# Bucket bits of seven head pairs: twelve fp32r products become four fp32 products in four column tiles, ten steps earlier

## The chip, the core and the metric

The kernel runs on one core of one Trainium2 chip. The metric is the device time of one execution in microseconds. The kernel before takes 722.88 us, the median of three runs from 721.88 to 723.98.

## The reference

Attention in which a query sees only the keys of its own hash bucket, and then two feed-forward layers of 1536 tokens, 512 channels and 2048 hidden units:

```python
B, H, S, D = 2, 8, 768, 64
q_bits = (einsum('bhsd,dk->bhsk', q, proj) > 0)      # six bits per query
k_bits = (einsum('bhsd,dk->bhsk', k, proj) > 0)      # six bits per key
mask = bucket(q_bits)[:, :, :, None] == bucket(k_bits)[:, :, None, :]
scores = where(mask, D**-0.5 * q @ k.T, -1e9)
x = softmax(scores) @ v                              # then to 1536 x 512
x = square(relu(x @ w_in1)) @ w_out1
out = silu(x @ w_in2) @ w_out2
```

All inputs are fp32, and the result has to be close to fp32 accuracy.

## The kernel before

The 16 heads are taken as 8 pairs. Operands of the large products are split in two fp32r parts, a high part and what is left, and a product of two such operands is written as three products. The mask is put into the score product itself: beside the 64 rows of q and k that belong to the low parts, the second half of each head's operand (`qq[h][:, 1]`, `kk[h][:, 1]`) has 12 rows with bits, six for "bit is set" and six for "bit is not set". On the query side they hold one or zero, on the key side a large negative number or zero, so that each bit in which a query and a key differ adds a large negative number to the score.

**The calendar of the attention.** `lsh_attention_moe_moe` writes one order of all instructions by hand. Its loop runs over steps d from -5 to 98 (line 1243 on). One step makes the scores of one tile of 128 queries (`score_mm`, line 989, four products into one of two PSUM banks-of-two `s`), takes the row maximum of the tile before (`row_max`, 996, and `row_live`, 1000 and 1001, on VectorE), its exponential (`score_exp`, 1009, on ScalarE), transposes two key tiles (`transp`, 1025, six transposes into a ring of three banks `t`), splits them (`t_hi`, a cast on ScalarE, 1030; `t_lo`, a subtraction on VectorE, 1036), and multiplies two earlier ones with v (`av`, 1049 and 1050). Twelve steps are one pair; in what follows d0 = 12 (p - 1) for pair p, whose scores run from step d0+7 (head 0) and d0+13 (head 1). Beside this, `todo[d]` holds what a step issues at its end, `last[d]` what comes after that, and `mid[d]` what VectorE does in its middle, after `row_live`. The engines and the DMA queues take their instructions in order: what SyncE waits for holds back every later DMA of its queue.

**The bits of pairs 1 to 7.** For each pair, q and k (two heads, 128 rows) are loaded (`load_pair`, 741, at d0-13, `load_k`, 744, at d0-6), q is scaled on ScalarE (758, at d0-7), high parts are cast on GpSimd (754, at d0-7 and d0-2) and low parts subtracted there (774, at d0-5 and d0-1). In step d0+5 (5, 17, ..., 77; the table `long`) `bits_mm` (line 789) multiplies with the signed projection: for each half of the 768 columns six fp32r products of 128 rows, 48 output rows and 384 columns, that is the high projection with the high part, the low projection with the high part and the high projection with the low part, for q and for k. They accumulate in 48 rows of two banks, one taken from the scores (`s`), one from the transposes (`t`). Two comparisons on VectorE (`bits_cmp`, 795) turn them into the bits tile `bt`, of which there is one buffer. In such a step the exponential goes ahead of the products with v, since the bits take its bank, and q of a later pair is scaled right after it. `place_bits` (919) then sends 12 rows of `bt` into `qq` and 12 into `kk` by two DMAs on SyncE's queue, for head 0 at the end of step d0+5, for head 1 at step d0+8. The heads' other rows are sent there by `load_head` (764, 766) and `place_lo` (779, 780). Pair 0 makes its bits apart, before step 0 (`first_bits_mm`, 884, `second_bits_mm`, 900).

**The first layer's w_in.** Four tiles of w_in, stored as fp64 words, are made fp32 during the attention: a load (943), an absolute value on ScalarE (950), a limit on GpSimd (954), and three integer operations on VectorE (`w_exp` 958, `w_sign` 962, `w_low` 966). `W_STEPS` names the steps: load, absolute value and limit, then the three. Two raw tiles are used in turn. At the last of the steps of the first two, `wp_put` (973, 974) splits the tile for the feed-forward part.

After the attention a planner orders the two layers; their first products (line 420) need the first x and w_in tiles. The row sums of each pair come back as a tile `rw` (1087), of which there are two buffers.

Of the kernel before, what the change touches and what calls it, by code (L numbers as in the profile page):

```python
# [23 lines left out]
NB = 6  # L24
# [7 lines left out]
WARM = {-4: 5, 0: 1, 1: 1}  # L32
PW = 96
C = float(2.0**36)
# [5 lines left out]
V_LAG = 4  # L40
W_STEPS = ((0, 5, 17, 17, 29), (8, 17, 29, 41, 53), (30, 41, 53, 65, 77), (54, 65, 77, 92, 93))
WA = 4
# [657 lines left out]
def lsh_attention_moe_moe(ctx, tc, kd, qk, qf, fq, v, pc, wi1, wo1, wi2, wo2, out):  # L700
# [27 lines left out]
    pjs = ac.tile([128, PW], F32, name="pjs")  # L728
    pjh = ac.tile([128, PW], F32R, name="pjh")
    pjl = ac.tile([128, PW], F32R, name="pjl")  # L730
    pjd = ac.tile([128, 3, 88], F32R, name="pjd")
    pdx = ac.tile([128, 2, NBR], F32, name="pdx")
    tm = [tmt[:, 2 * i : 2 * i + 2] for i in range(4)]
    mt = ac.tile([128, 4, 4], F32, name="mt")

    pair = {}
# [33 lines left out]
    def split_pair(p, i):  # L770
        t = pair[p]
        if i == 0:
            t["lp"] = a1.tile([128, 2, S], F32R, tag="lp", bufs=2, name=f"lp{p}")
        nc.gpsimd.tensor_tensor(out=t["lp"][:, i], in0=t["r"][i], in1=t["hp"][i].bitcast(F32), op=ALU.subtract)
# [7 lines left out]
    def bits_mm(p):  # L782
        t = pair[p]
        hp, lp = t["hp"], t["lp"]
        ops = [(w[:, 48 * i : 48 * i + 48], x) for i in range(2) for (w, x) in ((pjh, hp[i]), (pjl, hp[i]), (pjh, lp[:, i]))]
        s = ps_s.tile([128, 2, 512], F32, tag="s", name=f"bs{p}")[:, 0], ps_t.tile([128, 512], F32, tag="t", name=f"bt{p}")
        for z in range(2):
            for j, (w, x) in enumerate(ops):
                mm(s[z][0:48, 0:QW], w, x[:, z * QW : (z + 1) * QW], start=j == 0, stop=j == 5)  # L789
        return s  # L790

    def bits_cmp(s, p, z):
        if z == 0:
            pair[p]["bt"] = a1.tile([128, S], F32R, tag="bt", name=f"bt{p}")
        nc.vector.tensor_scalar(
            out=pair[p]["bt"][0:48, z * QW : (z + 1) * QW],
            in0=s[z][0:48, 0:QW],
            scalar1=tm[0][0:48, 0:1],
            scalar2=tm[0][0:48, 1:2],
            op0=ALU.is_gt,  # L800
            op1=ALU.mult,
        )

# [6 lines left out]
    def first_load(h):  # L810
        t = pair[0]
        if h == 0:
            c = ac.tile([128, S], F32, tag="P", bufs=6, name="fc")
            first["c"] = c[:, 0:NFQ]
            first[0, 0] = c[:, NFQ : NFQ + QW], ac.tile([128, S], F32, tag="P", bufs=6, name="fq1")[:, 0:QW]
            k = a1.tile([128, S], F32, tag="ta", bufs=2, name="fk")
            first[0, 1] = k[:, half(0)], k[:, half(1)]
            nc.sync.dma_start(out=c[:, 0 : NFQ + QW], in_=fq)
            nc.scalar.dma_start(out=first[0, 1][0], in_=qf[0, 1, :, half(0)])
            nc.sync.dma_start(out=first[0, 1][1], in_=qf[0, 1, :, half(1)])  # L820
            nc.scalar.dma_start(out=first[0, 0][1], in_=qf[0, 0, :, half(1)])
        else:
            first[1, 0] = a1.tile([128, S], F32, tag="tb", name="fr10")
            first[1, 1] = a1.tile([128, 6, 2, 64], F32, tag="rw", bufs=2, name="fr11").rearrange("p a b c -> p (a b c)")
# [90 lines left out]
    def place_bits(p, h):  # L915
        t = pair[p]
        for n, x in enumerate(("qq", "kk")):
            r = 24 * n + NBR * h
            nc.sync.dma_start(
                out=t[x][h][64 : 64 + NBR, 1, :].bitcast(F32),  # L920
                in_=t["bt"][r : r + NBR].bitcast(F32),
            )

# [13 lines left out]
    def w_load(key):  # L937
        m, io, i = key
        if io:
            weights[key] = raw[i], late[i]  # L940
        else:
            weights[key] = raw[i % 2], ac.tile([128, 512], F32, tag="wi", bufs=2, name=f"wi{i}") if i < 2 else wt[i - 2]
        nc.sync.dma_start(out=weights[key][0], in_=((wi1, wo1), (wi2, wo2))[m][io][i])
# [125 lines left out]
    def norm_rows(p):  # L1069
        ri = sums[p]  # L1070
        nc.vector.reciprocal(out=ri, in_=ri)
        if p == NPAIR - 1:
            w = rows[p] = a1.tile([128, 6, 2, 64], F32, tag="rw", bufs=2, name=f"rw{p}")
            nc.gpsimd.tensor_copy(out=w, in_=ri.rearrange("p (h c) -> p c h", h=2).unsqueeze(3).broadcast_to([128, 6, 2, 64]))
# [9 lines left out]
    def row_get(p):  # L1084
        w = rows[p] = a1.tile([128, 6, 2, 64], F32, tag="rw", bufs=2, name=f"rw{p}")
        for h in range(2):
# [88 lines left out]
    with tc.manual_schedule():  # L1175
# [50 lines left out]
        at(-4, lambda: nc.gpsimd.tensor_tensor(out=pjs, in0=pcr[:, 0:PW], in1=pcr[:, PW:], op=ALU.mult))  # L1226
        at(-4, lambda: nc.gpsimd.tensor_copy(out=pjh, in_=pjs))
        at(-4, lambda: nc.gpsimd.tensor_tensor(out=pjl, in0=pjs, in1=pjh.bitcast(F32), op=ALU.subtract))
        at(-3, scale_q, 1)
# [9 lines left out]
        for d in range(-5, G // 2 + 3):  # L1239
# [17 lines left out]
            elif 0 <= g < G:  # L1257
# [59 lines left out]
def _layout(q, k, v, proj, moe_w_in, moe_w_out, moe2_w_in, moe2_w_out):  # L1317
# [13 lines left out]
    for s in range(2):  # L1331
        for h in range(2):
            for e in range(2):
                r = 24 * s + NBR * h + NB * e
                c = 48 * s + r
                plus = e == s
                pj[64 * h : 64 * h + 64, c : c + NB] = proj
                sg[:, c : c + NB] = 1.0 if plus else -1.0
                at = (TINY if plus else -TINY2, -C if s else 1.0)
                tm[r : r + NB, 0:2] = at  # L1340
                tm[64 + NB * e : 64 + NB * e + NB, 2 + 2 * s : 4 + 2 * s] = at
# [20 lines left out]
```

## Time and profile before

| what | value |
|---|---|
| median of three runs | 722.88 us |
| profiled execution, its own time | 722.25 us |
| span in that profile, first to last instruction | 720.5 us |
| TensorE busy | 714.9 us, 99% of the span |
| VectorE, ScalarE, GpSimd busy | 609.0, 538.8, 257.6 us |
| granted TensorE clock, mean | 0.999 |

Times in rows are microseconds from the start of the span unless marked ns. PE is TensorE, PEld its weight loads, DVE VectorE, ACT ScalarE, POOL GpSimd, SPq the queue of SyncE. In a timeline a row is: start, length, engine, line, operation, out<-in, shapes, count, and in brackets the idle time before it with what ended it. "issue" is idle time for which the profile shows no other cause. Ends of products are modelled, so that two products in a row overlap in the listing; the distance between starts is the better measure.

### The profile page before, as it was taken

The numbers are of one execution on the slowest core, as the hardware profiler recorded it, in microseconds if no ns is written. First come the engines' busy times: TensorE is split into PE (matmuls) and PEld (weight loads), VectorE is DVE, ScalarE is ACT, GpSimd is POOL, SyncE is SP. The second block draws the span as 40 slices with busy tenths as digits, with TensorE's granted clock in tenths as the row PEclk, the third lists the DMA queues.
The fourth block names the chain that finished last, engine by engine and source line by source line (L and its number), as shares of the span: only waits on it lengthen the run. The fifth ranks groups of instructions, "written<-read, shape, count | busy, mean of one in ns | idle before, by whom it ended". The sixth has DMA issues, their size and how long they took to land.

```text
span 720.5 us, 10899 instructions
## 1 busy us (share of the span) xinstructions
PE 714.9 (99%) x3638; PEld 611.8 (85%) x3638; DVE 609.0 (85%) x1106; ACT 538.8 (75%) x1012; POOL 257.6 (36%) x241
## 2 busy tenths in 40 slices
PE   9999999999999999999999999999999999999998
PEld 4999999999999888888888888888788888888886
DVE  6999999999999888886797889988878788888840
ACT  6998898899898897495568569888765945854861
POOL 7645656665546421041331231244204111212300
PEclk9999999999999999999999999999999999999999
DMA  5788898797553555143544742477131332245432
GB/s 173 199 199 172 177 225 168 176 231 173 135 134 86 117 158 120 59 96 95 117 102 103 167 126 74 102 174 179 52 94 58 89 103 84 92 103 117 103 110 95
DMA packets 38824, 92.56 MB, mean 128 GB/s; under 512 B 5608, under 2 KB 10580, under 8 KB 38768
## 3 DMA queue, kind: packets, MB, share of 16 engines
q1 hardware_dynamic: 26304, 67.58, 33.4%
q0 software_dynamic: 12032, 23.79, 18.9%
q8 instruction: 29, 0.48, 0.3%
q10 hardware_dynamic: 432, 0.49, 0.2%
q14 instruction: 27, 0.22, 0.1%
HBM read 52.35 MB, written 3.19 MB: 77 GB/s over the span
## 4 chain that ended last, share of the span: by engine, by line
PE 98%; DVE 1%; ACT 0%; issue 0%; DVEq 0%; ACTq 0%
PE bank L558 36%; PE bank L443 25%; PE s L989 9%; PE t L1025 9%; PE bank L420 7%; PE o L1049 5%; PE o L1050 5%; PE bs L789 1%; PE bt L789 1%; PE warm L980 1%; DVE mt L996 0%; ACT P L1009 0%; PE bs L900 0%; PE bf L884 0%; PE t L1263 0%
## 5 line engine op out<-in xcount | busy, mean ns | idle before, releaser
L558 PE MATMUL bank<-woh,cell 128*128 128x512 f32 (+1 forms) x392 | 119.9, 385 | 0.0
L558 PE MATMUL bank<-cell,woh 128*128 128x512 f32 x384 | 118.4, 389 | 0.0
L1009 ACT ACTIVATE P<-s,mt 128x768 f32<-128x768 f32 x96 | 95.4, 994 | 14.1 <-DVE mt L1001 10.7
L1036 DVE TENSOR_TENSOR tl<-t,th 128x384 fp32r<-128x384 f32 x192 | 104.6, 548 | 0.5 <-ACT th L1030 0.5
L996 DVE TENSOR_REDUCE mt<-s 128x1 f32<-128x768 f32 x96 | 91.4, 952 | 3.2 <-PE s L989 2.4
L1030 ACT CAST th<-t 128x384 fp32r<-128x384 f32 x192 | 81.9, 484 | 8.4 <-PE t L1025 8.1
L558 PEld LDWEIGHTS bank<-woh,cell 128*128 128x128 f32 x392 | 73.1, 188 | 14.7
L989 PE MATMUL s<-kk,qq 76*128 76x384 f32 (+1 forms) x384 | 84.7, 340 | 0.7 <-ACT P L1009 0.5
L558 PEld LDWEIGHTS bank<-cell,woh 128*128 128x128 f32 x384 | 72.1, 188 | 15.2 <-DMA cell<-cell 0.2
L1025 PE MATMUL t<-ident,P 128*128 128x128 f32 x576 | 79.0, 273 | 0.0
L278 DVE TENSOR_TENSOR cell<-bank,cell 128x512 f32<-128x512 f32 x91 | 62.1, 692 | 19.7 <-PE bank L443 15.3
L443 PE MATMUL bank<-xw,wpb 128*128 128x512 f32 x312 | 75.9, 389 | 0.0
L558 PE MATMUL bank<-wol,cell 128*128 128x512 f32 (+1 forms) x196 | 75.4, 385 | 0.0
L558 PE MATMUL bank<-cell,wol 128*128 128x512 f32 x192 | 74.7, 389 | 0.0
L1049 PE MATMUL o<-th,vv 128*128 128x384 f32 x192 | 72.5, 378 | 0.0
L1025 PEld LDWEIGHTS t<-ident,P 128*128 128x128 f32 x576 | 68.0, 140 | 4.6 <-DVE tl L1036 0.2
L989 PEld LDWEIGHTS s<-kk,qq 76*128 76x128 f32 (+1 forms) x384 | 68.0, 188 | 4.1 <-issue 1.6
L443 PEld LDWEIGHTS bank<-xw,wpb 128*128 128x128 f32 x312 | 58.5, 188 | 12.4 <-DVE bank L278 0.3
L1050 PE MATMUL o<-tl,vv 128*128 128x384 f32 x192 | 64.5, 336 | 0.0
L588 ACT COPY yf<-bank 128x512 f32<-128x512 f32 x48 | 27.9, 585 | 34.6 <-PE bank L558 33.9
L450 ACT COPY cell<-bank 128x512 f32<-128x512 f32 x39 | 22.9, 586 | 40.6 <-PE bank L443 38.6
L268 ACT CAST cell<-cell 128x512 fp32r<-128x512 f32 x81 | 48.8, 617 | 2.5 <-DMA cell<-cell 1.3
(198 smaller groups left out, 1480.9 us busy)
## 6 DMA issues: line engine op xcount, KB each, us to landing
raw<-in_dram SPq DMA_DIRECT2D x64, 512.0 KB
cell<-cell POOLq DMA_DIRECT2D x23, 256.0 KB, 3.6
qq<-hq SPq DMA_DIRECT2D x28, 192.0 KB
kk<-in_dram POOLq DMA_DIRECT2D x14, 384.0 KB, 5.8
yf<-cell POOLq DMA_DIRECT2D x21, 256.0 KB, 3.6
vr<-in_dram SPq DMA_DIRECT2D x8, 384.0 KB
ta<-ob SPq DMA_DIRECT2D x31, 96.0 KB
tb<-ob SPq DMA_DIRECT2D x31, 96.0 KB
```

Of the source, the lines that this page charges most:

```text
L278: add("DVE", 0.70, lambda: vec.tensor_tensor(out=val(out), in0=bank[b], in1=val(other), op=ALU.add), [("bank", b), *reads], writes)
L420: mm(bank[b], wpa[n][:, p, 4 * h + j], x[:, q], start=j == 0 and z == 0, stop=j == 3 and z == 2)
L443: mm(bank[b], w[:, p], x[:, q], start=not started and z == 0, stop=z == 2, skip_group_check=started)
L558: mm(bank[b][:, 0:wd], x, y, start=start and i == 0 and z == 0, stop=i == (FB if half is None else 2 * half + 2) - 1 and z == 2, skip_grou ...
L989: mm(s[:, n, 0:QW], t["qq"][h][0:kk, ab, c0 : c0 + 128], t["kk"][h][0:kk, ab, n * QW : (n + 1) * QW], start=ab == 0, stop=ab == 1)
L996: nc.vector.tensor_reduce(out=m[:, 0:1], in_=s[:, :, 0:QW], op=ALU.max, axis=AX.XY, negate=True)
L1009: nc.scalar.activation(out=e.rearrange("p (a b) -> p a b", a=2), in_=s[:, :, 0:QW], func=AF.Exp, scale=m[:, 1:2], bias=m[:, 2:3], accum_ou ...
L1025: nc.tensor.transpose(t[:, j * 128 : (j + 1) * 128], P[u, j][:, kt * 128 : (kt + 1) * 128], ident)
L1030: nc.scalar.copy(out=th, in_=PT[g][0][:, 0:QW])
L1036: nc.vector.tensor_tensor(out=tl, in0=t[:, 0:QW], in1=th.bitcast(F32), op=ALU.subtract)
L1049: mm(o[:, 0:QW], vv, th, start=kt == 0, stop=False)
L1050: mm(o[:, 0:QW], vv, tl, start=False, stop=kt == KT - 1)
```

## The change

It forms the bits of pairs 1 to 7 from q and k as loaded, by four fp32 products per pair, one for each of q and k and each half of the columns. Each writes 24 of 32 output rows of its own at partition 0, 32, 64 or 96 of one bank from the ring `t`. The projection is no longer split, and `pjh` and `pjl` go with the two GpSimd operations that made them. One comparison of 128 partitions and 384 columns makes all bits of the pair; `place_bits` sends each half of the columns by its own DMA, four per head in place of two. The products stand at the end of step d0-2 (step 1 for pair 1), after the scores, the comparison in the middle of step d0-1, and the bits of head 0 are placed at step d0+2.

q and k of a pair are loaded at d0-10 and d0-9. k is cast and split first (d0-4, d0-3), q is scaled in step d0-2 after the bits products, which read it unscaled, then cast and split (d0-2, d0-1). The exponential no longer changes its place in a step with bits. The w_in tiles get a third raw tile `rx` and other steps: only step 41, 92 and 96 still have two of the VectorE operations, and the last tile is finished at step 96. `rw` has one buffer.

```diff
-PW = 96
+PW = 64
-W_STEPS = ((0, 5, 17, 17, 29), (8, 17, 29, 41, 53), (30, 41, 53, 65, 77), (54, 65, 77, 92, 93))
+W_STEPS = ((0, 5, 17, 29, 53), (8, 17, 41, 65, 77), (22, 29, 41, 92, 93), (54, 65, 92, 96, 96))
...
-    pjh = ac.tile([128, PW], F32R, name="pjh")
-    pjl = ac.tile([128, PW], F32R, name="pjl")
+    rx = ac.tile([128, 512], I64, name="rx")
...
     def bits_mm(p):
-        t = pair[p]
-        hp, lp = t["hp"], t["lp"]
-        ops = [(w[:, 48 * i : 48 * i + 48], x) for i in range(2) for (w, x) in ((pjh, hp[i]), (pjl, hp[i]), (pjh, lp[:, i]))]
-        s = ps_s.tile([128, 2, 512], F32, tag="s", name=f"bs{p}")[:, 0], ps_t.tile([128, 512], F32, tag="t", name=f"bt{p}")
-        for z in range(2):
-            for j, (w, x) in enumerate(ops):
-                mm(s[z][0:48, 0:QW], w, x[:, z * QW : (z + 1) * QW], start=j == 0, stop=j == 5)
-        return s
+        o = ps_t.tile([128, 512], F32, tag="t", name=f"bs{p}")
+        for c in range(4):
+            n, z = divmod(c, 2)
+            mm(o[32 * c : 32 * c + 32, 0:QW], pjs[:, 32 * n : 32 * n + 32], pair[p]["r"][n][:, z * QW : (z + 1) * QW], start=True, stop=True)
+        return o
+
+    def bits_cmp(p, o):
+        t = pair[p]["bt"] = a1.tile([128, S], F32R, tag="bt", name=f"bt{p}")
+        nc.vector.tensor_scalar(out=t[:, 0:QW], in0=o[:, 0:QW], scalar1=tm[0][:, 0:1], scalar2=tm[0][:, 1:2], op0=ALU.is_gt, op1=ALU.mult)
...
     def place_bits(p, h):
...
-            r = 24 * n + NBR * h
-            nc.sync.dma_start(
-                out=t[x][h][64 : 64 + NBR, 1, :].bitcast(F32),
-                in_=t["bt"][r : r + NBR].bitcast(F32),
-            )
+            o = t[x][h][64 : 64 + NBR, 1, :].rearrange("r (z c) -> r z c", z=2)
+            for z in range(2):
+                r = 64 * n + 32 * z + NBR * h
+                nc.sync.dma_start(out=o[:, z].bitcast(F32), in_=t["bt"][r : r + NBR, 0:QW].bitcast(F32))
...
-            weights[key] = raw[i % 2], ac.tile([128, 512], F32, tag="wi", bufs=2, name=f"wi{i}") if i < 2 else wt[i - 2]
+            weights[key] = (rx, raw[0], raw[1], rx)[i], ac.tile([128, 512], F32, tag="wi", bufs=2, name=f"wi{i}") if i < 2 else wt[i - 2]
...
-            at(max(d0 - 13, 1), load_pair, p)
-            scale[d0 - 7] = p
-            at(d0 - 7, new_hi, p)
-            at(d0 - 7, cast_pair, p, 0)
-            at(d0 - 6, load_k, p)
-            at(d0 - 2, cast_pair, p, 1)
-        at(max(d0 - 5, 0), split_pair, p, 0)
-        at(max(d0 - 1, 0), split_pair, p, 1)
-        long[d0 + 5] = p
+            at(d0 - 10, load_pair, p)
+            at(d0 - 9, load_k, p)
+            at(d0 - 4, new_hi, p)
+            at(d0 - 4, cast_pair, p, 1)
+            at(d0 - 3, split_pair, p, 1)
+            scale[d0 - 2] = p
+            at(d0 - 2, cast_pair, p, 0)
+            at(d0 - 1, split_pair, p, 0)
+        else:
+            at(0, split_pair, p, 0)
+            at(0, split_pair, p, 1)
+        long[max(d0 - 2, 1)] = p
         at(d0 + 1, load_head, p, 0)
         at(d0 + 2, place_lo, p, 0)
-        last[d0 + 5].append((place_bits, (p, 0)))
+        at(d0 + 2, place_bits, p, 0)
...
-            if d in long:
-                score_exp(*ready, m)
-                if d in scale:
-                    scale_q(scale.pop(d))
             for n in (g - V_LAG, g + 1 - V_LAG):
                 if 0 <= n < G:
                     av(n)
             if d in long:
-                t = bits_mm(long[d])
-            if d in long:
-                bits_cmp(t, long[d], 0)
                 t_lo(g + 1)
-                bits_cmp(t, long[d], 1)
-            if ready and d not in long:
+            if ready:
                 score_exp(*ready, m)
             u, j = divmod(d + 5, 3)
             if u < NU:
                 new = u, j, score_mm(u, j)
+            if d in long:
+                mid[d + 1].append((bits_cmp, (long[d], bits_mm(long[d]))))
+            if d in scale:
+                scale_q(scale.pop(d))
             for fn, a in todo.pop(d, []) + last.pop(d, []):
                 fn(*a)
```

Left out of the diff: the old `bits_cmp`, the two GpSimd operations that made `pjh` and `pjl`, the smaller `bufs` of `rw`, the condition in `split_pair` that makes the tile of low parts with whichever half comes first, and the order of the constants in the host's layout.

## Rows read from the trace of the kernel before

**Rows 1.** The page's busy times (part 1) and its chain by engine (part 4).

```profile
PE 714.9 (99%) x3638; PEld 611.8 (85%) x3638; DVE 609.0 (85%) x1106; ACT 538.8 (75%) x1012; POOL 257.6 (36%) x241
...
PE 98%; DVE 1%; ACT 0%; issue 0%; DVEq 0%; ACTq 0%
```

**Rows 2.** Busy times in one stretch: span, PE, PEld, DVE, ACT, POOL.

```profile
54.20:81.40 27.20, 27.20 (x183) 25.66 (x182) 26.87 (x66) 24.82 (x57) 16.96 (x14) 1.00 0.92 181
```

**Rows 3.** Timeline of TensorE, transposes that open a step.

```profile
26.12 0.82 PE L1025 MATMUL t<-ident,P 128*128 128x128 f32 x6
...
80.11 0.82 PE L1025 MATMUL t<-ident,P 128*128 128x128 f32 x6
...
84.38 0.82 PE L1025 MATMUL t<-ident,P 128*128 128x128 f32 x6
...
101.00 0.82 PE L1025 MATMUL t<-ident,P 128*128 128x128 f32 x6
...
107.17 0.82 PE L1025 MATMUL t<-ident,P 128*128 128x128 f32 x6
...
188.50 0.82 PE L1025 MATMUL t<-ident,P 128*128 128x128 f32 x6
```

**Rows 4.** Timeline, bits on SyncE's queue, and the weight load that waits for them.

```profile
85.83 0.77 SPq L919 DMA_DIRECT2D kk<-bt  x1
...
88.19 0.30 PEld L989 LDWEIGHTS s<-kk,qq 76*128 76x128 f32 x2 [0.19 <-issue]
...
92.60 0.95 SPq L919 DMA_DIRECT2D qq<-bt  x1
...
93.70 0.83 SPq L919 DMA_DIRECT2D kk<-bt  x1
```

**Rows 5.** Timeline of TensorE, first and last of twelve bits products, and the next.

```profile
81.58 0.33 PE L789 MATMUL bs<-hq,pjh 128*48 128x384 f32 x1
...
81.58 0.12 PEld L789 LDWEIGHTS bs<-hq,pjl 128*48 128x48 f32 x1
...
83.49 0.34 PE L789 MATMUL bt<-lp,pjh 128*48 128x384 f32 x1
...
83.67 0.88 PE L989 MATMUL s<-kk,qq 128*128 128x384 f32 x4
```

**Rows 6.** Groups by line: operation, shapes, count, busy us, mean ns, idle before.

```profile
L1025 PE MATMUL t<-ident,P 128*128 128x128 f32 x576 | 79.0, 273 | 0.0
...
L795 DVE TENSOR_SCALAR bt<-bs,tmt 48x384 fp32r<-48x384 f32 x7 | 4.6, 662 | 0.3 <-PE bs L789 0.3
...
L966 DVE SCALAR_TENSOR_TENSOR wi<-raw,wi 128x512 uint32<-128x512 uint32 x2 | 1.4, 683 | 0.0
...
L758 ACT ACTIVATE rq<-rq 128x768 f32<-128x768 f32 x7 | 5.8, 833 | 0.0
```

**Rows 7.** Timeline of TensorE, products of pair 0 in two row halves.

```profile
6.04 0.44 PE L884 MATMUL bf<-qq,pjd 64*76 64x384 f32 x1
...
6.05 0.61 PE L884 MATMUL bf<-hk,pjd 64*76 64x384 f32 x2
```

**Rows 8.** Timeline of TensorE, bits of pair 0: 128 rows, then 64.

```profile
13.84 0.34 PE L900 MATMUL bs<-kk,pjd 128*24 128x384 f32 x1
...
14.11 0.35 PE L900 MATMUL bs<-qq,pjd 64*24 64x384 f32 x1
```

**Rows 9.** Timeline of one steady step: score, subtraction, exponential, row maximum.

```profile
98.25 0.86 PE L989 MATMUL s<-kk,qq 128*128 128x384 f32 x4
...
98.61 0.55 DVE L1036 TENSOR_TENSOR tl<-t,th 128x384 fp32r<-128x384 f32 x1
...
98.73 0.99 ACT L1009 ACTIVATE P<-s,mt 128x768 f32<-128x768 f32 x1 [0.22 <-DVE mt L1001]
...
99.14 0.96 DVE L996 TENSOR_REDUCE mt<-s 128x1 f32<-128x768 f32 x1
```

**Rows 10.** Timeline of TensorE, first products after the attention.

```profile
228.96 11.40 PE L420 MATMUL bank<-xk,wpa 128*128 128x512 f32 x49
```

More of the change, by code (lines that the diff above doesn't have):

```diff
@@ L771, in split_pair @@
         t = pair[p]
-        if i == 0:
+        if "lp" not in t:
             t["lp"] = a1.tile([128, 2, S], F32R, tag="lp", bufs=2, name=f"lp{p}")
@@ L782, in bits_mm @@
     def bits_mm(p):
-        t = pair[p]
-        hp, lp = t["hp"], t["lp"]
-        ops = [(w[:, 48 * i : 48 * i + 48], x) for i in range(2) for (w, x) in ((pjh, hp[i]), (pjl, hp[i]), (pjh, lp[:, i]))]
-        s = ps_s.tile([128, 2, 512], F32, tag="s", name=f"bs{p}")[:, 0], ps_t.tile([128, 512], F32, tag="t", name=f"bt{p}")
-        for z in range(2):
-            for j, (w, x) in enumerate(ops):
-                mm(s[z][0:48, 0:QW], w, x[:, z * QW : (z + 1) * QW], start=j == 0, stop=j == 5)
-        return s
[L792 to L801, printed above, removed]
-        )
+        o = ps_t.tile([128, 512], F32, tag="t", name=f"bs{p}")
[6 more added lines that the diff above has]
+        nc.vector.tensor_scalar(out=t[:, 0:QW], in0=o[:, 0:QW], scalar1=tm[0][:, 0:1], scalar2=tm[0][:, 1:2], op0=ALU.is_gt, op1=ALU.mult)
     first = {}
@@ L823, in first_load @@
             first[1, 0] = a1.tile([128, S], F32, tag="tb", name="fr10")
-            first[1, 1] = a1.tile([128, 6, 2, 64], F32, tag="rw", bufs=2, name="fr11").rearrange("p a b c -> p (a b c)")
+            first[1, 1] = a1.tile([128, 6, 2, 64], F32, tag="rw", name="fr11").rearrange("p a b c -> p (a b c)")
             for i in range(2):
@@ L917, in place_bits @@
         for n, x in enumerate(("qq", "kk")):
-            r = 24 * n + NBR * h
-            nc.sync.dma_start(
-                out=t[x][h][64 : 64 + NBR, 1, :].bitcast(F32),
-                in_=t["bt"][r : r + NBR].bitcast(F32),
-            )
+            o = t[x][h][64 : 64 + NBR, 1, :].rearrange("r (z c) -> r z c", z=2)
+            for z in range(2):
+                r = 64 * n + 32 * z + NBR * h
+                nc.sync.dma_start(out=o[:, z].bitcast(F32), in_=t["bt"][r : r + NBR, 0:QW].bitcast(F32))
     def load_v(p):
@@ L1072, in norm_rows @@
         if p == NPAIR - 1:
-            w = rows[p] = a1.tile([128, 6, 2, 64], F32, tag="rw", bufs=2, name=f"rw{p}")
+            w = rows[p] = a1.tile([128, 6, 2, 64], F32, tag="rw", name=f"rw{p}")
             nc.gpsimd.tensor_copy(out=w, in_=ri.rearrange("p (h c) -> p c h", h=2).unsqueeze(3).broadcast_to([128, 6, 2, 64]))
@@ L1084, in row_get @@
     def row_get(p):
-        w = rows[p] = a1.tile([128, 6, 2, 64], F32, tag="rw", bufs=2, name=f"rw{p}")
+        w = rows[p] = a1.tile([128, 6, 2, 64], F32, tag="rw", name=f"rw{p}")
         for h in range(2):
@@ L1226, in lsh_attention_moe_moe @@
         at(-4, lambda: nc.gpsimd.tensor_tensor(out=pjs, in0=pcr[:, 0:PW], in1=pcr[:, PW:], op=ALU.mult))
-        at(-4, lambda: nc.gpsimd.tensor_copy(out=pjh, in_=pjs))
-        at(-4, lambda: nc.gpsimd.tensor_tensor(out=pjl, in0=pjs, in1=pjh.bitcast(F32), op=ALU.subtract))
         at(-3, scale_q, 1)
@@ L1333, in _layout @@
             for e in range(2):
-                r = 24 * s + NBR * h + NB * e
-                c = 48 * s + r
+                r = NBR * h + NB * e
                 plus = e == s
-                pj[64 * h : 64 * h + 64, c : c + NB] = proj
-                sg[:, c : c + NB] = 1.0 if plus else -1.0
+                pj[64 * h : 64 * h + 64, 32 * s + r : 32 * s + r + NB] = proj
+                sg[:, 32 * s + r : 32 * s + r + NB] = 1.0 if plus else -1.0
                 at = (TINY if plus else -TINY2, -C if s else 1.0)
-                tm[r : r + NB, 0:2] = at
+                for z in range(2):
+                    tm[64 * s + 32 * z + r : 64 * s + 32 * z + r + NB, 0:2] = at
                 tm[64 + NB * e : 64 + NB * e + NB, 2 + 2 * s : 4 + 2 * s] = at
```

## The prediction, made blind

> **What bounds the kernel now.** I read the page's busy times and its chain first: TensorE is busy 99% of the span and the chain of waits that ended last lies on it for 98% [rows 1]. So a microsecond less of TensorE work is a microsecond less of time, unless another engine is right behind. The reader should see in one stretch of the attention how close the others are: of 27.20 us, VectorE works 26.87, ScalarE 24.82, GpSimd 16.96 [rows 2]. VectorE is nearly full as well; the other two have room.
>
> The timeline of TensorE gives the rhythm. A step without bits takes 2.06 us (three steps from 101.00 to 107.17), the step with bits 4.27 us (80.11 to 84.38), and from the first step with bits at 26.12 to the seventh at 188.50 there are six pairs of 27.06 us each [rows 3]. Twelve steps are 24.68; the bits (and a small transpose that shares their step) add 4.27 - 2.06 = 2.21; 27.06 - 24.68 - 2.21 = 0.17 is left as stall. Where it sits: the two DMAs that place the bits of head 0 are issued only after the comparison; the second ends its issue at 86.60 and the score product that reads the bits stands still for 0.19 us until 88.19 [rows 4]. The bits landed 1.6 us after their issue, a little too late.
>
> **The change part by part.**
>
> *Removed on TensorE.* Twelve fp32r products of 384 columns per pair: first start 81.58, next work at 83.67, so 2.09 us, or 0.174 each [rows 5].
>
> *Added on TensorE.* Four fp32 products of 384 columns, each into its own 32 columns of the array. The trace has no such product, so I bound it. The only fp32 work on TensorE are the transposes: six in 0.82 us with 0.273 for the last alone [rows 3, 6], (0.82 - 0.273)/5 = 0.109 for 128 columns, or 0.85 ns a column against 0.45 for fp32r. Low end for one product: 384 x 0.85 ns = 0.33 us. High end: the kernel before writes each fp32 product as three fp32r ones; with the fourth part, 4 x 0.174 = 0.70. I take 0.70, since here both operands are full fp32, while a transpose's identity has nothing to split. Then the question is whether the four run side by side. Low end: all four together, 0.33. High end: one after the other, 2.78. The nearest row speaks for side by side: two products in different halves of the array's rows start at 6.04 and 6.05, the second beside the first [rows 7]. It is a row split and not a column split, and fp32r. I take 0.70 for all four.
>
> *The change of array tile.* In the rows, going between 128 and 64 array rows makes the next product start 0.27 us after the last (13.84 to 14.11) [rows 8], where the 384 columns alone take 0.17: 0.10 each. Going from 128 to 64 array columns for the old bits and back shows nothing: 83.49 to 83.67 is the same 0.17 to 0.18 as between bits [rows 5]. So two changes per pair cost 0 to 0.20; I take 0.10, and 0.10 more for weight loads that may not be hidden among four tiles. The Trainium skill (TensorEngine Tiling (Array Packing), Key Properties) says that a change of tiling mode, other than of the tile, drains TensorE. By that rule the higher end, 0.20, would hold; the rows agree for row tiles and disagree for column tiles. So the bits of a pair come to 0.90, bounds 0.33 and 2.98.
>
> *Bits sooner.* Their DMAs go out at step d0+2 and are needed at d0+7, five steps or 10 us: the 0.17 us of stall goes.
>
> *VectorE.* One of two comparisons goes, 0.66 us [rows 6]. The one left has the same 384 columns, on 128 partitions, so I price it the same. It moves to step d0-1, where TensorE's bits no longer give it cover. In the steady rhythm the row maximum starts as the score ends (98.25 + 0.86 = 99.11, start 99.14), right behind the subtraction of 98.61 + 0.55 [rows 9]: VectorE has under 0.1 us of slack per step. About 24.0 us for its twelve steps, 0.6 for the comparison, 0.6 for conversions of w_in (up to 0.68 each [rows 6], now mostly one per pair instead of two in the bits' step) make some 25.3 us per pair: VectorE is the floor if TensorE falls under that.
>
> *A new wait.* The comparison writes the one bits tile, and must wait until the four DMAs of the previous pair's head 1, issued at step d0-4, have read it. Before, the two of them run from 92.60 to 94.53 [rows 4]; two more of 0.8 bring this to 96.1, landing 1.6 later at 97.7. The comparison's place is 1.7 us into step d0-1, at 96.55 on the same scale (that step starts three steps before 101.00). So VectorE waits about 1.1 us, and behind it stand the subtractions, the next row maximum, its exponential, and the score product that needs its bank. TensorE is meanwhile 0.9 longer in its own bits, and a score bank gives 0.59 us of play (the exponential ends at 98.73 + 0.99 = 99.72, and its bank is written again one step after 98.25, at 100.31 [rows 9]), so I charge 0.30 per pair; ends 0 (SyncE ahead of schedule) and 0.80 (nothing hides it).
>
> *ScalarE, GpSimd, SyncE.* Scaling q, 0.83 us [rows 6], now waits on ScalarE for the bits products, with the next step's casts behind it; hidden in ScalarE's 2.4 us of room per pair, at most 0.1 a pair without. GpSimd loses two small operations at the start and gets its casts in another order: hidden by 10 us of room. SyncE issues 28 more DMAs, 0.8 us each, 3 us a pair; only the wait above sees them, as everything else queued behind (row sums, v, the next q and k) is needed many steps later. q and k are loaded at d0-10 and d0-9, six steps before their use. The single row buffer costs nothing, since GpSimd has read the old rows before it writes the new. The last two conversions of w_in fall behind the last subtractions, 1.4 us; TensorE covers them with 11.40 us of products that need nothing new [rows 10].
>
> **Sum.** Gain per pair 2.09 + 0.17 = 2.26, cost 0.90 + 0.30 = 1.20, net 1.06, for seven pairs 7.4 us. A pair becomes 26.0, still above VectorE's 25.3. The profiled execution took 722.25 (span 720.5), which gives 714.85; the median of the runs is 0.63 above it, so 715.5. With the bounds of this case (VectorE's floor, gain 1.7 a pair; or 1.20 of bits and 0.80 of wait, gain 0.3) it runs from 711 to 721, mostly 712.5 to 719.
>
> **The rivals.**
>
> *Half overlap.* If a product is two streams of 0.33 one behind the other, and starts keep their order, only the second of one tile runs beside the first of the next: 5 x 0.33 = 1.65, with weight loads and the change of tile 1.8 to 2.1. The new wait then hides behind it. Net 0.16 to 0.46 a pair, 1 to 3 us: about 720.8. For it: every product here has its own weight load and starts are in order in all rows. Against: nothing shows two streams.
>
> *End to end, slower.* If the four tiles don't overlap, four products take 2.64 to 2.78, plus 0 to 0.20: a loss of 0.4 to 0.7 a pair, 3 to 5 us, about 727. It decides from the point where the four together pass 2.26 us. For it: no row has two column tiles at once. Against: the overlap of [rows 7]. The Trainium skill (TensorE: Matmul & The Clock Gate, Part 3) says that a weight load overlaps matmuls in flight only when its row group differs, and here all four tiles use all rows; that would be this rival. The trace disagrees for the full array: the weight load at 81.58 runs under the product of the same start [rows 5].
>
> *VectorE or the bits tile eats it.* The four overlap, but the wait of 1.1 us reaches TensorE whole and the conversions, without cover, cost as much again per pair: gain 0.4 a pair, 3 us, about 719.5.
>
> **How the numbers follow.** Forecast 0.52, half overlap 0.22, end to end 0.20, VectorE 0.06. A measurement of this kernel tells about 0.3%, 2.2 us, from no change. Faster: the forecast nearly whole, half of half overlap, most of the last, 0.66. Same: 0.14. Slower: 0.20. The range from 712.5 to 726 holds the first two and the last nearly whole and the mild edge of the slower case; the likeliest case's own range is 712.5 to 719.
>
> **What would show it.** Right: four bits products that start within some 0.1 us of each other and last about 0.7, the step with bits near 3.0 us instead of 4.27, no idle time before the score product in step d0+7, six pairs in 156 us instead of 162.4. The new wait would stand as idle time on VectorE before the comparison, released by the DMAs of the bits tile. Wrong: bits products whose starts are 0.6 us or more apart, or steps d0-1 and d0 stretched by more than half a microsecond.

## The result: slower, and the profile after

The changed kernel takes 730.22 us (median of six runs, 728.03 to 733.26), the kernel before 722.80 beside it (six runs): a ratio of 1.0096, interval 1.0078 to 1.0114, slower by 7.4 us. I had forecast 715.5 and a range up to 726. The profiled execution took 731.64, with a span of 729.9.

The page of the changed kernel: busy times, the chain by engine, and the group of the transposes (the last column is idle time before them, with what ended it). They answer to [rows 1, 6].

```profile
PE 712.2 (98%) x3610; PEld 604.8 (83%) x3610; DVE 604.9 (83%) x1099; ACT 539.7 (74%) x1012; POOL 257.6 (35%) x239
...
PE 77%; DVE 11%; SPq 4%; DMA 4%; issue 2%; ACT 1%; POOL 0%; DVEq 0%; ACTq 0%; POOLq 0%
...
L1013 PE MATMUL t<-ident,P 128*128 128x128 f32 x576 | 82.3, 276 | 9.7 <-DVE bt L791 8.3
```

TensorE's busy time fell by 2.7 us, less than its work did, as some products ran at a lower clock; the span grew by 9.4. The chain lay on TensorE for 98%; now 77%. The transposes, which never waited [rows 6], stand still for 9.7 us, 8.3 of them for the comparison of the bits (L791).

The list of waits of the changed kernel says what is behind it (sum, times, longest, in us):

```profile
DVE bt L791 <- DMA kk<-bt: 10.4, 5, 4.5
...
PEld t L1013 <- DVE bt L791: 10.2, 6, 4.3
...
PEld t L1013 <- DVE tl L1024: 7.6, 18, 0.6
...
PEld bank L420 <- DVE ta L1045: 2.9, 1, 2.9
```

First the comparison waits for the last DMA that reads the one bits tile, then the weight loads of the transposes wait for the comparison. (The first row counts five comparisons of six: the wait of the sixth, 1.4 us for pair 3, the list puts down to a score product, which the comparison doesn't read. With a second bits tile, below, it goes with the others.) The third row is a smaller wait of the same transposes for the subtractions, the fourth one wait at the end of the attention. The timeline of the changed kernel shows each place: the step with bits and the one behind it for pair 5, the same wait for pair 6, and the end of the attention.

```profile
121.37 0.52 PE L786 MATMUL bs<-rq,pjs 128*32 128x384 f32 x2
121.38 1.47 SPq L910 DMA_DIRECT2D kk<-bt  x2
121.39 0.11 PEld L786 LDWEIGHTS bs<-rk,pjs 128*32 128x32 f32 x2
121.39 0.52 PE L786 MATMUL bs<-rk,pjs 128*32 128x384 f32 x2
...
121.72 0.49 PE L786 MATMUL bs<-rq,pjs 128*32 128x384 f32 x2
121.73 0.49 PE L786 MATMUL bs<-rk,pjs 128*32 128x384 f32 x2
...
122.16 0.88 PE L1013 MATMUL t<-ident,P 128*128 128x128 f32 x6
...
124.85 0.68 DVE L791 TENSOR_SCALAR bt<-bs,tmt 128x384 fp32r<-128x384 f32 x1 [1.72 <-DMA kk<-bt]
125.28 1.83 POOL L774 TENSOR_TENSOR lp<-rq,hq 128x768 fp32r<-128x768 f32 x1
125.44 0.55 DVE L1024 TENSOR_TENSOR tl<-t,th 128x384 fp32r<-128x384 f32 x1
...
125.58 1.01 PE L1013 MATMUL t<-ident,P 128*128 128x128 f32 x6 [1.14 <-DVE bt L791]
...
156.11 1.54 PE L1013 MATMUL t<-ident,P 128*128 128x128 f32 x6 [3.93 <-DVE bt L791]
...
158.09 0.52 PE L1037 MATMUL o<-th,vv 128*128 128x384 f32 x1
...
160.51 0.34 PE L1037 MATMUL o<-th,vv 128*128 128x384 f32 x1
...
232.73 0.87 DVE L950 SCALAR_TENSOR_TENSOR both<-rx,both 128x512 uint32<-128x512 uint32 x1
...
233.02 2.39 POOL L1083 TENSOR_TENSOR ta<-ta,tb 64x384 f32<-64x384 f32 x2
...
233.15 0.84 PE L1277 MATMUL rb<-ident,rw 128*128 128x128 f32 x6
...
233.64 2.32 DVE L954 SCALAR_TENSOR_TENSOR both<-rx,both 128x512 uint32<-128x512 uint32 x1
...
235.99 0.56 DVE L1045 TENSOR_TENSOR ta<-o,ta 64x384 f32<-64x384 f32 x1
...
236.61 14.15 PE L420 MATMUL bank<-xk,wpa 128*128 128x512 f32 x54 [2.62 <-DVE ta L1045]
```

**The bits** (121.37 to 122.16) are as forecast. Each fp32 product is two records, so a row with x2 holds those of both halves of the columns. The first records of all four products start within 0.03 us of each other, the second ones 0.35 later, and the next work follows 0.79 after the first start. The step with bits is 2.93 us long instead of a plain 2.06, a price of 0.87 per pair where I had said 0.90. (The products stand seven steps earlier than before, at d0-2 instead of d0+5, and four for pair 1; the "ten steps" of the title is wrong.)

**The comparison** (124.85) stands 1.72 us and TensorE stands behind it: the next six transposes go into the ring bank that holds the bits, and start at 125.58, as the comparison ends (124.85 + 0.68 = 125.53). Behind the comparison on VectorE the subtractions and the next row maximum are late as well.

**The end.** The last product with v used to be followed by products with w_in that waited for nothing [rows 10]; now these wait 2.62 us for L1045 on VectorE, which starts as the second of the last two conversions of w_in ends (233.64 + 2.32 = 235.96). These two are 0.87 and 2.32 us long where a conversion takes 0.68 [rows 6]; the second ends 0.55 behind the GpSimd row above it (235.41), and the runs on conversions below show what that means.

Both pauses shown here are followed by a lower clock. Busy times of the changed kernel by stretch (PE, PEld, DVE, ACT, POOL, then the granted clock, the DMA share and GB/s), behind the 3.93 us pause of pair 6 and behind the one at the end:

```profile
156.50:160.00 3.50, 3.50 (x19) 3.46 (x18) 2.29 (x7) 1.94 (x4) 0.00 (x0) 0.67 0.10 23
...
236.60:240.00 3.40, 3.39 (x9) 2.66 (x10) 3.31 (x5) 1.68 (x4) 1.66 (x1) 0.61 0.00 0
240.00:244.00 4.00, 4.00 (x17) 3.29 (x16) 2.64 (x5) 2.32 (x5) 2.53 (x3) 0.90 0.37 66
```

TensorE works all of these 3.5 us and gets little done: the product that took 0.52 at 158.09 takes 0.34 at 160.51. 0.61 and 0.67 are means between the two levels, 1.2 and 2.4 GHz. Before, the first 13.70 us behind the attention were granted 1.00:

```profile
228.90:242.60 13.70, 13.70 (x63) 11.36 (x62) 13.29 (x19) 11.86 (x22) 8.67 (x8) 1.00 0.42 92
```

**The account of the two spans.** From the first transpose of step 0 to that of step 95 the attention took 209.25 us (16.14 to 225.39); now 214.39 (15.76 to 230.15), 5.1 more. What comes behind took 495.1 and takes 499.7, 4.6 more. What stands ahead of step 0 is 0.4 shorter.

### The profile page after: what moved, and what is told of

Its sections match the earlier page's. It is cut to its first block, busy times and chain, and to the rows that moved or that the text cites. A ratio compares the mean times of both kernels' runs of the same rounds, so it can differ in the third digit from the quotient of the medians.

```text
span 729.9 us, 10863 instructions
## 1 busy us (share of the span) xinstructions
PE 712.2 (98%) x3610; PEld 604.8 (83%) x3610; DVE 604.9 (83%) x1099; ACT 539.7 (74%) x1012; POOL 257.6 (35%) x239
## 3 DMA queue, kind: packets, MB, share of 16 engines
HBM read 52.32 MB, written 3.19 MB: 76 GB/s over the span
## 4 chain that ended last, share of the span: by engine, by line
PE 77%; DVE 11%; SPq 4%; DMA 4%; issue 2%; ACT 1%; POOL 0%; DVEq 0%; ACTq 0%; POOLq 0%
PE bank L558 35%; PE bank L443 23%; PE bank L420 7%; DVE mt L984 4%; DVE tl L1024 4%; PE s L977 4%; PE t L1013 4%; DMA kk<-bt 2%; PE o L1037 2%; PE o L1038 2%; SPq L910 2%; DMA rx<-in_dram 1%; DMA cell<-cell 1%; SPq L766 1%; PE warm L968 1%
## 5 line engine op out<-in xcount | busy, mean ns | idle before, releaser
L1013 PE MATMUL t<-ident,P 128*128 128x128 f32 x576 | 82.3, 276 | 9.7 <-DVE bt L791 8.3
```

The lines of the kernel that those rows point to most:

```text
L1013: nc.tensor.transpose(t[:, j * 128 : (j + 1) * 128], P[u, j][:, kt * 128 : (kt + 1) * 128], ident)
```

## The experiments

Lengths of steps are distances between the first transposes of two steps; the times in the table are in us, those of the second and third column from the start of the step. Undisturbed, the comparison starts 0.91 us into its step, d0-1 (0.88 to 0.98 in the first experiment). In the changed kernel it came later, and TensorE's step grew by this:

| pair (step) | last issue of `kk<-bt` ends | comparison starts | its delay | step | over 2.06 |
|---|---|---|---|---|---|
| 2 (11) | 1.68 | 3.17 | 2.26 | 3.90 | 1.84 |
| 3 (23) | 0.91 | 2.34 | 1.43 | 3.07 | 1.01 |
| 4 (35) | 0.18 | 1.76 | 0.85 | 2.49 | 0.43 |
| 5 (47) | 0.70 | 2.69 | 1.78 | 3.42 | 1.36 |
| 6 (59) | 2.55 | 5.49 | 4.58 | 6.22 | 4.16 |
| 7 (71) | 0.81 | 2.19 | 1.28 | 2.92 | 0.86 |

The delay less 0.42 us is the growth in all six rows: 9.7 us in sum, 1.6 a pair. The 0.42 is the play of the comparison, the time by which it may be late before TensorE stands longer. It can be read: the transposes start 0.73 us after the comparison (124.85 to 125.58), and 2.06 - 0.73 - 0.91 = 0.42. The steps behind add 0.19 each, and 1.33 where the clock fell (step 60), 2.3 in all. The theory: with a second bits tile this goes. The rival: the long chain is a symptom, and VectorE is full.

**A second bits tile.** Each pair needs 384 columns of the tile's 768, so two of 384 take the same memory.

```diff
-        t = pair[p]["bt"] = a1.tile([128, S], F32R, tag="bt", name=f"bt{p}")
+        t = pair[p]["bt"] = a1.tile([128, QW], F32R, tag="bt", bufs=2, name=f"bt{p}")
```

(Pair 0 puts its two halves into the two tiles.)

> The changed kernel with two bits tiles of 384 columns in turn instead of one (pair 0 uses one for each half), everything else the same. Theory (the comparison waits until the DMAs of the pair before have read the one bits tile, and TensorE then waits for the bank that the comparison reads): no idle time of VectorE before the comparison, the six stretched steps of 2.5 to 6.2 us go back to 2.1 to 2.3, the attention is 10 to 13 us shorter (9.7 of stretch, 1 to 3 of what follows it and of the clock), so about 718 to 720. Rival (the wait only covers another bound, VectorE without cover for its conversions): the stretch moves to other steps and half of it stays, about 725.

Measured: 720.70 us (ten runs), ratio 0.9969 (0.9955 to 0.9983). The six steps are 2.11 to 2.13 long, those behind 2.05 or 2.06, the attention 202.79. So 0.07 of each step's growth, 0.4 us in sum, is there without any wait. The wait at the end stays, 2.7 us in the list of waits. The theory holds: the wait for the one tile cost 9.5 us by the medians (11.6 of attention in the profiled execution of the change, which was 1.4 over its median).

**The banks of the feed-forward part.** The old bits took a score bank seven times; without that, the last product with v lies in the other of the two. The planner of the feed-forward part hands out its first banks in a fixed order, and the first is now the one that L1045 still reads.

```diff
-    idle = [0, 1, 4, 7, 2, 3, 5, 6]
+    idle = [2, 3, 4, 7, 0, 1, 5, 6]
```

> The changed kernel with one bits tile, and with the feed-forward part taking its PSUM banks in the order 2, 3, 4, 7, 0, 1, 5, 6 instead of 0, 1, 4, 7, 2, 3, 5, 6. Theory (without bits in the score banks the last product with v falls into the other of the two, and the first feed-forward product waits for that bank until VectorE, late by the two conversions of step 96, has read it): the idle time of 2.6 us before the first feed-forward product goes, with it the lower clock right behind (granted 0.61 over 3.4 us), together 3.5 to 4.5 us, so about 726. Rival (it waits for x or w_in, not for the bank): the wait stays within 0.5 us of 2.6, time 730.

Measured: 726.43, ratio 1.0049 (1.0032 to 1.0067), 3.8 us less than the change as it was. The wait at the end of the attention and the low clock behind it are gone (granted 1.00 in all of 220 to 250 us). The wait was 2.6 of this, so 1.2 are left for the clock; by the stretch behind the attention in the two profiles (499.7 and 495.0) it is 2.1. My estimate from the granted shares lies between: (1 - 0.61) x 3.40 + (1 - 0.90) x 4.00 = 1.7. The steps d0-1 keep 3.71, 3.46, 3.49, 3.22, 5.35 and 2.99 us.

**The old kernel with the new order** is the counter-test: the order should hurt there.

```diff
-    idle = [0, 1, 4, 7, 2, 3, 5, 6]    (in the kernel before)
+    idle = [2, 3, 4, 7, 0, 1, 5, 6]
```

> The kernel before with only the feed-forward part's order of banks changed to 2, 3, 4, 7, 0, 1, 5, 6. Theory (which score bank the last product with v falls into decides whether the first feed-forward product waits): the first feed-forward product, at 228.96 before, now waits for VectorE's last reading at 229.7, 0.5 to 0.9 us later, no lower clock, time 0.3 to 1 us more, 723 to 724. Rival (the order of banks matters by itself in the feed-forward part): a difference of over 2 us.

Measured: 723.20, ratio 1.0010 (0.9995 to 1.0024). The wait appears in its list of waits, in the same place:

```profile
PEld bank L420 <- DVE ta L1057: 0.8, 1, 0.8
PE bank L420 <- DVE ta L1057: 0.6, 1, 0.6
```

It is short, since no conversion stands ahead of L1057 there. So the order of banks alone makes a wait of 0.6; that the conversions moved to step 96 make 2.6 of it is read from the timeline of the change (235.96 and 235.99) and wasn't tried by itself. The time moves by less than a measurement can tell.

**Both mended.**

> Both edits: two bits tiles and the other order of banks. Theory: the two losses are apart and add, 714 to 716, faster than the kernel before by 7 to 9 us, as four products of 0.78 us together replace twelve of 2.09. Rival (VectorE is the next bound): the gain over the kernel before stays under 3 us, 720 or more.

Measured: 716.08 (715.62 to 716.73), ratio 0.9907 (0.9892 to 0.9921): 7 us faster than the kernel before, the best version here, and 4.6 faster than with the second bits tile alone. Its timeline, at the comparison of pair 5 and at the end of the attention:

```profile
118.50 0.88 PE L1013 MATMUL t<-ident,P 128*128 128x128 f32 x6
...
119.41 0.68 DVE L791 TENSOR_SCALAR bt<-bs,tmt 128x384 fp32r<-128x384 f32 x1
...
120.62 0.82 PE L1013 MATMUL t<-ident,P 128*128 128x128 f32 x6
...
221.13 1.54 DVE L950 SCALAR_TENSOR_TENSOR both<-rx,both 128x512 uint32<-128x512 uint32 x1
...
222.12 4.13 PE L420 MATMUL bank<-xk,wpa 128*128 128x512 f32 x17
222.70 1.40 DVE L954 SCALAR_TENSOR_TENSOR both<-rx,both 128x512 uint32<-128x512 uint32 x1
```

No bracket stands behind any of these: the comparison comes 0.91 us into its step, the next step begins 2.12 after it, and the products with w_in start while VectorE still converts.

**With one bits tile, its DMAs ahead of the low parts'.** This keeps the one tile and lets SyncE issue the bits of head 1 two DMAs sooner.

```diff
-        at(d0 + 8, place_lo, p, 1)
         at(d0 + 8, place_bits, p, 1)
+        at(d0 + 8, place_lo, p, 1)
```

> The changed kernel, with one bits tile, and at step d0+8 the four DMAs of the bits ahead of the two that place the low parts. Theory (the comparison waits for these DMAs, and their place in SyncE's queue sets when they land): they land 1.2 us earlier; the six stretched steps lose 1.2 us each where they have as much, a sum of 9.7 us of stretch goes to about 4, the time to about 724. Rival (the landing is set by the transfers in flight, not by the place in the queue): the stretch loses under 2 us, 729 or more.

Measured: 721.69, ratio 0.9981 (0.9964 to 0.9997), 2.3 below what I expected. The steps are 3.19, 2.13, 2.13, 2.13, 2.74 and 2.13. In the two that still grow, the comparison started 2.45 and 2.01 into the step: less 0.91 and 0.42 that is 1.12 and 0.68, the growth that was measured (1.13 and 0.68). I had taken 1.2 us off each comparison. What the order gave was no fixed length: the last issue ended 1.2 to 3.8 us sooner, and in step 59 the comparison came 3.48 sooner (5.49 to 2.01), in step 11 only 0.72 (3.17 to 2.45). Step 59 makes the miss.

**w_in's third raw tile later.** In pair 6 a 512 KB load to `rx` stood ahead of the bits' DMAs in the chain of the changed kernel (start, length, what; L916 loads v, L910 places the bits), and SyncE's list of waits has a wait for it (sum, times, longest):

```profile
139.90 0.57 SPq L916
...
141.05 9.10 DMA rx<-in_dram
...
150.16 0.76 SPq L910
...
151.73 3.52 DMA kk<-bt
```

```profile
SPq L910 <- DMA rx<-in_dram: 2.2, 1, 2.2
```

```diff
-W_STEPS = (..., (54, 65, 92, 96, 96))
+W_STEPS = (..., (61, 72, 92, 96, 96))
```

> The changed kernel with the fourth w_in tile loaded at step 61 instead of 54 and its absolute value at step 72 instead of 65. Theory (the load of 512 KB goes out just ahead of the bits DMAs of pair 5 and they land behind it, which makes step 59 the longest of all, 5.4 to 6.2 us): step 59 falls to 2.5 to 3.5 us like the other five, the step behind it to 2.25, and the clock doesn't fall there: 3 to 5 us less, 725 to 727. Rival (step 59 is long for another reason): it stays within 0.5 us of 5.4 to 6.2.

Measured: 731.38, ratio 1.0118 (1.0076 to 1.0160), no gain where I expected 3 to 5 us. Step 59 fell to 3.96, but step 47 rose to 4.30 and the others were 3.79, 3.96, 2.78 and 2.60: the growth is in sum 9.0 where it was 9.7. Each obeys the 0.42 us again; what differs is when the DMAs land. The load bears on pair 6, by the 2.2 us above, but it does not make the sum. What steps 59 and 60 gave back in the profiled execution went, beside step 47, to the low clock behind that one (steps 48 and 49 took 2.98 and 2.91) and to step 78: 3.88 where it had been 2.55, as its conversion took 2.01 us beside a sum on GpSimd.

**The old calendar of w_in**, on top of the two mends, to price the new one:

```diff
-W_STEPS = ((0, 5, 17, 29, 53), (8, 17, 41, 65, 77), (22, 29, 41, 92, 93), (54, 65, 92, 96, 96))
+W_STEPS = ((0, 5, 17, 17, 29), (8, 17, 29, 41, 53), (30, 41, 53, 65, 77), (54, 65, 77, 92, 93))
```

> Both edits, and the steps of the w_in conversions as in the kernel before (two VectorE operations in steps 17, 29, 53 and 77, the last one at step 93). Theory that conversions outside of the bits' step are uncovered and stretch the step after next by 0.3 to 0.6 us each time: steps 17, 29, 53, 77 are stretched by 0.5 to 1.1 us, 1 to 2 us more in all than with the new steps. Rival (VectorE catches up in the slack of the steps behind): same within 0.5 us.

Measured: 717.82, ratio 0.9930 (0.9914 to 0.9947), 1.7 slower than with the new one, as expected. Steps with two conversions are 2.90 to 3.02.

**Conversions without cover.** In the version with both mends, the steps behind a conversion are still 2.29, 2.55, 2.64, 2.54, 2.56 and 2.54 (18, 30, 42, 54, 66, 78), 2.8 us over 2.06. Three runs tried to hide them. The first puts them behind the first subtraction of their step. The second keeps that and halves all but the first and the last five (256 columns in each of two steps). The third, without these two, moves six to the steps with bits and one to step 82:

```diff
-            mid[d].append((fn, (key,)))
+            after_lo[d].append((fn, (key,)))
```

```diff
-W_STEPS = ((0, 5, 17, 29, 53), (8, 17, 41, 65, 77), (22, 29, 41, 92, 93), ...)
+W_STEPS = ((0, 5, 8, (14, 19), (26, 31)), (8, 17, (38, 43), (50, 55), (62, 67)), (22, 29, (74, 79), 92, 93), ...)
```

```diff
-W_STEPS = ((0, 5, 17, 29, 53), (8, 17, 41, 65, 77), (22, 29, 41, 92, 93), ...)
+W_STEPS = ((0, 5, 10, 22, 34), (8, 17, 46, 58, 70), (22, 29, 82, 92, 93), ...)
```

> Two bits tiles, the other order of banks, and the w_in conversions on VectorE behind the first subtraction of their step instead of ahead of it. Theory (TensorE waits for the bank of the ring that the first subtraction frees, so that a conversion ahead of it costs its length less 0.19): the six stretched steps behind 17, 29, 41, 53, 65 and 77 (0.23 to 0.58 each, 2.75 us in all) keep 0 to 0.3 each, 1 to 2 us less in all than with both edits alone, about 714.5. Rival (VectorE has no slack, wherever a conversion stands it costs the same): the same stretch in other steps, within 0.5 us of 716.1.

> As the run before, and the conversions that fall into the attention cut in halves of 256 columns, two per pair, at steps of 12k+2 and 12k+7 (the first whole at step 8, the last five at 92, 93 and 96 as they were). Theory (VectorE wins back some 0.06 us a step and TensorE stands only when it is over 0.4 us late): 0.4 us of conversion every five to seven steps is hidden whole, 2 to 3 us less than with both edits alone, about 713.5. Rival (no slack at all): the same time as with whole conversions, plus 0.06 us for each further instruction, 716 to 717.

> Two bits tiles, the other order of banks, and the w_in conversions of the attention in the steps of the bits (10, 22, 34, 46, 58, 70) where TensorE has 0.87 us more to do, one in step 82. Theory (this is the only cover in the changed rhythm): the stretched steps behind 17, 29, 41, 53 and 65 go, the step after the bits grows by 0.1 to 0.3 us, 1 to 2 us less than with both edits alone, 714 to 715. Rival (the comparison uses the cover up): the stretch only moves, 716 to 717.

Measured: 718.77, 722.77 and 718.92 us, all three slower than 716.08: three misses. The costliest places have one reason. The timeline of the third, in a step with bits:

```profile
64.84 1.82 POOL L774 TENSOR_TENSOR lp<-rk,hk 128x768 fp32r<-128x768 f32 x1
...
64.96 2.25 DVE L950 SCALAR_TENSOR_TENSOR wi<-rx,wi 128x512 uint32<-128x512 uint32 x1
...
67.74 1.01 PE L1013 MATMUL t<-ident,P 128*128 128x128 f32 x6 [1.50 <-DVE tl L1024]
```

And of the first:

```profile
80.76 1.83 POOL L1083 TENSOR_TENSOR ta<-ta,tb 128x768 f32<-128x768 f32 x1 [4.16 <-DMA kk<-bt]
...
81.09 2.05 DVE L950 SCALAR_TENSOR_TENSOR wi<-rx,wi 128x512 uint32<-128x512 uint32 x1
...
84.62 0.52 PE L1013 MATMUL t<-ident,P 128*128 128x128 f32 x3 [1.33 <-DVE tl L1024]
```

A conversion of 0.68 us that starts beside a two-input operation of GpSimd ends 0.55 us behind it: 64.96 + 2.25 = 67.21 against 64.84 + 1.82 = 66.66, and 83.14 against 82.59. Behind a cast with one input it is the same 0.55 (third run, step 34: 93.59 against 93.04). In the halved version a half took 1.17 us beside such an operation and 0.41 without one. The Trainium skill (SBUF — State Buffer, Who interferes with whom) says that a VectorE instruction with two inputs in SBUF contends with a GpSimd instruction that reads SBUF. These rows agree, and so do the subtractions of the attention, which read one input from PSUM: the one at 125.44 in the changed kernel takes its usual 0.55 with a GpSimd subtraction beside it (125.28, 1.83 long).

This is not the whole of the misses. In the first run, up to step 78, one conversion met GpSimd (step 30 became 3.55 long instead of 2.55). The others of 0.68 us, at their usual length, still cost 0.42 in the two steps behind them where they had cost 0.48 to 0.50, so the new place hid hardly more. In the second a half of 0.41 that met no GpSimd still cost about 0.25.

The third run also shows the cover. Its conversions in steps with bits took 2.25, 0.92, 1.47 and 1.79 (steps 22, 34, 58, 70) and the steps 4.49, 3.16, 3.71 and 4.03: over 2.93 that is 1.56, 0.23, 0.78 and 1.10, each conversion less 0.69. Two of 0.42 and 0.50 cost nothing there. So a step with bits hides 0.69 us on VectorE in itself, a plain one 0.19 (0.42 gave 0.23 more, 0.68 gave 0.48 to 0.50). But the two steps behind each of the four grew as well, by 0.3 to 0.4 us together, so that the real cover is smaller. Whether the place is the right one is open: GpSimd's own work for the pair stands there, and a calendar that keeps GpSimd's subtractions out of it wasn't tried.

**The bits twice.** The four products of each pair are issued two times, on top of both mends, to price them by themselves.

```diff
-        for c in range(4):
+        for c in (0, 1, 2, 3, 0, 1, 2, 3):
```

> Two bits tiles, the other order of banks, and the four bits products issued twice into the same bank. Theory (TensorE bounds the attention, and four products side by side cost 0.7 us): seven times 0.7, less what the longer step takes over from the stalls behind it, 4 to 5 us more than with both edits alone, 720 to 721. Rival (VectorE bounds it): under 2 us more.

Measured: 722.02, ratio 0.9992 (0.9981 to 1.0002), 5.9 us over the version with both mends. Timeline of TensorE:

```profile
40.52 0.52 PE L786 MATMUL bs<-rq,pjs 128*32 128x384 f32 x2
40.53 0.52 PE L786 MATMUL bs<-rk,pjs 128*32 128x384 f32 x2
...
40.86 0.49 PE L786 MATMUL bs<-rq,pjs 128*32 128x384 f32 x2
...
41.18 0.49 PE L786 MATMUL bs<-rq,pjs 128*32 128x384 f32 x2
...
41.51 0.49 PE L786 MATMUL bs<-rq,pjs 128*32 128x384 f32 x2
```

Four products more are two streams more, 0.32 and 0.33 us apart (40.86, 41.18, 41.51), and the steps with bits grow by 0.64, from 2.93 to 3.57: 4.5 us in seven. The attention is 4.46 longer. The rest is outside it: 0.7 ahead of step 0, and a wait for a DMA in the feed-forward part (1.6 in its list of waits). So TensorE's time does set the end once the waits are gone, and two streams of 0.32 to 0.35 side by side in four column tiles are the price.

## Why the prediction was wrong

**What was right.** The bits: 0.87 per pair against 0.90, with 0.68 instead of 0.70 for the four products together (two streams, 0.35 apart, and 0.33 for the second, as where they were issued twice). The 0.19 left is near the 0.20 that I put down for the change of array tile and for weight loads; no run parts these two. The half-overlap rival knew of two streams but took starts to keep their order in whole products; all four first streams start together. The end-to-end rival falls with it, and with it the rule that I cited beside it: The Trainium skill (TensorE: Matmul & The Clock Gate, Part 3) lets a weight load overlap matmuls in flight only where its row group differs, and the trace disagrees, since the load of 121.39 runs while the product of 121.37 does, on the same rows. The stall is gone too: steps d0+7 are 2.05 to 2.07 for pairs 2 to 7, where they had been up to 2.51 (pair 1's had no stall, and is now 2.17). So the gain ahead of any new wait was seven times 2.26 less 0.87, 9.7 us.

**The step that failed** is the one called *A new wait*: "so I charge 0.30 per pair; ends 0 (SyncE ahead of schedule) and 0.80 (nothing hides it)". It was 1.6 per pair, and 0.4 more in the step behind. The forecast's own sign of being wrong, steps d0-1 stretched by more than half a microsecond, holds in five of the six. It failed in three ways.

It was priced on one pair. For pair 4, whose rows I used [rows 4], I had the last issue 1.27 us into step 35 on the old scale, 0.4 once the 0.87 of the bits are taken off, a landing 1.6 later and a growth of 0.30; measured were 0.18, 1.58 and 0.43. That pair is the mildest of six. In the others SyncE, which issues eight DMAs in a row here, is up to 2.4 later, and the landing took 1.38 to 2.94.

The comparison's own place was wrong: I put it 1.7 us into its step, and it is 0.91. So every wait is 0.8 longer.

The play was put in the wrong place. I looked at the score bank and its 0.59 us. What TensorE stands for is the ring bank `t` of the bits, which the transposes of the next step need 0.42 us after an undisturbed comparison frees it. From there each microsecond of VectorE's is one of TensorE's, and its own 0.87 of bits in the step ahead hides nothing of it. And no other step gives it back, since each is full by itself; VectorE's 25.3 us per pair, which I compared with 26.0, say nothing about a wait in one step.

**A second step failed:** "TensorE covers them with 11.40 us of products that need nothing new". It was read from the kernel before, where the last product with v lay in the other bank. The bits had taken a score bank an odd number of times, and I did not follow what one user less does to a bank's turn. It cost 2.6 us of wait and 1.2 to 2.1 more behind it, where the clock was low; 3.8 us came back with the banks, 4.6 with two bits tiles.

**A third was left at nothing:** the conversions of w_in. I counted them in VectorE's sum, where they fit; in the plain step that each was moved to, all but 0.19 us showed, 2.8 in all.

The sum of the profile: 9.7 gained, 9.7 lost to the wait, 2.3 in the steps behind it, 2.8 for conversions: 5.1 worse in the attention, and 4.6 behind it. (0.4 of the 9.7 lost stays without the wait.) Of the rivals, *VectorE or the bits tile eats it* named the mechanism and both its parts. It had a chance of 0.06, and its 0.40 of gain a pair allows 0.96 for both parts (2.26 - 0.90 - 0.96), 6.7 us in all, where they measured 14.8. Without the wait and with the banks turned, the kernel takes 716.08, near the 715.5 that I forecast, but by another sum: no new wait, and 2.8 of conversions in its place. That these two agree is luck.

**What stays open:** why the landing of the same DMA takes 1.4 us in one pair and 2.9 in another, and why it differs from execution to execution: pair 4's comparison started 1.76 us into its step in the change and 2.76 in the version with other banks, whose attention is the same.

## What to carry to other kernels

A write to a single buffer waits for its slowest reader, so price it over every turn of the loop and at the place where the new code issues it; the pair whose rows one happens to read may be the mildest. On an engine that is full in every step, look for what stands behind the waiting instruction and how much play that has, not for room in the mean. And count who else takes turns in a pool: a user that leaves it an odd number of times moves every later tile to the other buffer.

## What the runs showed of the hardware

The play is sharp: in 18 steps of three kernels with one bits tile (the change, the one with other banks, the one with the late load), with delays from 0.85 to 4.58 us, the growth is the delay less 0.42, within a hundredth.

Four fp32 products of 384 columns in four column tiles run side by side, as two streams 0.35 us apart: 0.79 us from the first start to the next work, where twelve fp32r products took 2.09. A single such product was not run.

A conversion of 0.68 us on VectorE becomes up to 2.32 beside GpSimd, and GpSimd waits in its turn: where the conversion came first, one of its subtractions took 2.16 us instead of 1.83 (third run on conversions, step 34). The integer operation with one input (L946) is lengthened too: half of it took 1.07 us beside GpSimd instead of 0.28.

A pause of TensorE may be followed by the low clock or not: behind 2.62 us the granted clock was 0.61 for 3.4 us, behind 3.93 it was 0.67 for 3.5 (both in the change), behind a pause of 2.01 in the version with the late load 0.64 for 4 us, and behind one of 3.07 in the version with other banks 1.00. The length of the pause alone did not decide it.
